# Another order of the same opening steps in a fused windowed-attention and gated-MLP kernel

## The chip, the core and the metric

The kernel runs on one core of a Trainium2 chip. The metric is the device time of one execution in microseconds (us). Three runs of the kernel before gave 309.06, 309.11 and 309.75 us; their median is 309.11 us. One more execution was recorded by the hardware profiler; its span, from the first to the last instruction, is 306.3 us.

The engines go by short names: PE is TensorE, ACT is ScalarE, DVE is VectorE, POOL is GpSimd, SP is SyncE, which here only issues DMA. Each engine works off its own list of instructions in order, and an instruction waits until what it needs is there. PEld stands for the loading of weights into PE.

## The reference, cut to what matters

Batch is 8, with 8 heads, 576 positions and a head dimension of 64. A position attends to itself and the 63 before it. The result, with heads laid side by side, is x: 4608 rows of 512. Then follows a two-layer block with `g = h * cos(h)` between the layers.

```python
scores = scale * np.matmul(q, k.transpose(0, 1, 3, 2))
rel = pos[:, None] - pos[None, :]
mask = (rel >= 0) & (rel < window)           # window = 64
scores = np.where(mask, scores, -1000000000.0)
scores = scores - np.max(scores, axis=-1, keepdims=True)
attn = np.exp(scores)
attn = attn / (np.sum(attn, axis=-1, keepdims=True) + 1e-09)
attn_out = np.matmul(attn, v)
x = attn_out.transpose(0, 2, 1, 3).reshape(B * S, H * D)
h = x @ w_in                                  # 512 x 2048
g = h * np.cos(h)
out = g @ w_out                               # 2048 x 512
```

## The kernel before, in words

**Tiles.** The 4608 rows of x are worked in nine tiles of 512 rows. A tile needs x (attention for its rows), sixteen blocks of h (128 columns of w_in each, from four products over the four quarters of the 512 inputs), the cosine as a sine with a shifted argument on ACT, the gate `h * sin` on DVE, and then four blocks of 128 output rows, each a sum of sixteen products with w_out. While PE works on the products of tile t, a plan with written times puts the attention of a later batch between them. From tile 1 on (lines 579 to 618) nothing is changed.

**Attention.** The eight heads are taken as four pairs. 64 query positions of one pair are a *unit*: two heads of 64 rows make 128 rows, against two blocks of 64 keys. Up to four units form a *group* that shares one PSUM bank. Groups 0 to 7 are batch 0, pair p and half g (n = 2p + g); group 8 is the last block of positions of batch 0; groups 9 to 18 are batch 1. Groups 9 to 16 are needed for tile 1, two for each pair; 17 and 18 for tile 2.

**The opening.** Everything up to the end of tile 0, and the attention of batch 1 beside it, is not planned but written out as a list of steps, `FIRST` (line 50). Its order is the order of instructions on each engine; the list is one sequence for all engines, so a step's place counts only against the other steps of its own engine. The last letter of a step picks the engine: `a` ACT, `d` DVE, `p` POOL, `s` SP (a copy by DMA); a last digit of `s`, `h`, `Gs` and `o.0` picks one of five PSUM banks. The names:

- `Lq0.p`, `Lk0.p`, `Lq1.p`, `Lk1.p`: load q or k of batch 0 or 1 for pair p; issued by POOL and converted to bf16 on the way (line 165), except pair 0 of batch 0, which SP loads unconverted (line 171) and `cq`, `ck` convert. `Lq2.c`, `Lk2.c` load pieces of batch 2 (line 182).
- `Lv0.c`, `Lv1.c`: load 128 positions of v of batch 0 or 1 (line 188); `Lwi.i`, `Lwo.i`: a quarter of w_in or w_out (lines 204, 207). All these are issued by POOL.
- `io`, `mk`, `mc`: build the mask, by two steps on POOL (line 143), five small instructions on DVE (147 to 151) and three casts on ACT (155).
- `tq.p`, `tk.p` (batch 0), `Tq.p`, `Tk.p` (batch 1): transposes on PE (line 216, 18 instructions each); `pq`, `pk`, `Pq`, `Pk`: the copy out of PSUM (lines 234, 236, or the copy helper, line 137).
- `s.p.g` scores, `m.p.g` negated row maximum on DVE (319), `e.p.g` exponentials on ACT (336), `i.p.g` reciprocals on DVE (346), `n.p.g` the product with them (353), `w.p.g` transposed weights on PE (364), `c.p.g` their copy out of PSUM. For groups 8 to 18 the same steps are `Gs`, `Gm` (mask added on DVE, 324), `Ge`, `Gi`, `Gn`, then `Gw` and `Gp` (groups 8, 15, 16) or `Gc` (the others), a transposing DMA issued by SP (367).
- `zA`, `zB`, `zC`, `yA`, `yB`, `y`: v also has to lie shifted by 64 rows; these copy halves of the loaded tiles of batch 0 (`z`) and batch 1 (`y`).
- `v.a.g` (403): products of weights with v for pairs 2a, 2a + 1 and half g; `x.a.g`: the copy to x. `V.p`, `X.p` (384): the same for tile 1, pair p.
- `h.g.f` (417): eight products for half g (256 rows) of tile 0 and two blocks of h; `S.g.f` the sine (423), `g.g.f` the gate (429). `h.0.f` needs `x.0.0` and `x.1.0`, and quarter f // 2 of w_in.
- `o.q.m` (436): quarter q of the sum for output rows m; `oc.m` its copy. `tb`, `tb2` change ACT's function table. `ms.p` clears a tile that later batches use (546).

**Buffers that can hold PE up.** Scores, h and outputs share five PSUM banks, one buffer each, so a product into a bank waits for the last reader of what was there. Transposes and attention outputs rotate through three more banks. In tile 1 five blocks of h fit in the banks before the first gate has to free one. Of POOL's loads the ninth waits, in the trace, until the first has landed (`POOL q L165 <- DMA q<-in_q_dram`), and so on.

Of the kernel before, what the change touches and what calls it, by code (L numbers as in the profile page):

```python
# [648 lines left out]
```

## Time and profile before

| | |
|---|---|
| median of three runs | 309.11 us |
| span of the profiled execution | 306.3 us |
| busy: PE, DVE, ACT, POOL | 296.2, 228.5, 234.3, 192.5 us |
| PE waits for its first input until | 4.19 us |
| first product of tile 0's h (`h.0.0`, line 417) | 21.18 us |
| first product of tile 1's h (line 453) | 57.17 us |
| last instructions of PE (line 465) | from 299.90 us |

The profiler gives no time for the profiled execution other than its span: 306.3 us are 2.8 us less than the median of the runs, and what lies before the first and behind the last instruction is not in the trace. Times in the profile are microseconds from the start of the span unless marked ns. A row of the timeline has the start, the length, the engine, the line of the kernel, the operation, output and input, how many instructions were merged, and in brackets how long the engine sat idle before and for whom it waited. A row of a group has the busy time, the mean length of one instruction in ns, and the idle time before them. Matmuls overlap, so a row's length is longer than the distance to the next.

### The profile page before, as it was taken

The page shows a single profiled execution, that of the slowest core. Times are in us where ns is not written, and L with a number is a line of the kernel's source. Part 1 is how long each engine was busy: PE and PEld are TensorE (multiplying, and loading weights), DVE is VectorE, ACT ScalarE, POOL GpSimd, SP SyncE. Part 2 cuts the span into 40 slices and gives each one's busy share as a digit, 9 for nine tenths or more (in the row PEclk, how much of TensorE's full clock was granted, in tenths as well). Part 3 has the DMA queues.
Part 4 walks back from the last instruction along what each step waited for, and adds up shares of the span by engine and source line. Part 5 has one row for each costly group of instructions (what it writes and reads, how often), then busy time and mean ns, then how long its engine had stood idle before and what let it go on. Part 6 is the DMA issues. An engine that isn't in the chain of part 4 may idle for free.

```text
span 306.3 us, 7904 instructions
## 1 busy us (share of the span) xinstructions
PE 296.2 (97%) x2616; PEld 159.0 (52%) x2616; DVE 228.5 (75%) x908; ACT 234.3 (76%) x785; POOL 192.5 (63%) x228
## 2 busy tenths in 40 slices
...
GB/s 146 179 212 192 200 180 130 121 149 191 226 113 116 175 223 80 121 133 232 125 121 137 231 143 104 157 221 148 86 137 107 169 78 141 2 68 71 1 67 70
DMA packets 159945, 42.14 MB, mean 138 GB/s; under 512 B 148256, under 2 KB 155168, under 8 KB 159904
## 3 DMA queue, kind: packets, MB, share of 16 engines
...
HBM read 36.70 MB, written 9.44 MB: 151 GB/s over the span
## 4 chain that ended last, share of the span: by engine, by line
PE 90%; POOL 4%; DMA 2%; DVE 1%; ACT 1%; issue 1%; POOLq 0%; DVEq 0%; ACTq 0%
PE h_ps L453 35%; PE out_ps L609 35%; PE h_ps L417 5%; PE s_ps L303 4%; PE out_ps L436 4%; PE o_ps L384 3%; DMA k<-in_k_dram 2%; POOL w L353 2%; PE tq_ps L219 1%; POOL v L188 1%; PE out_ps L465 1%; PE s_ps L309 1%; PE tw_ps L364 1%; POOL w_in L204 1%; ACT e L336 1%
## 5 line engine op out<-in xcount | busy, mean ns | idle before, releaser
L609 PE MATMUL out_ps<-w_out,gT 128*128 128x512 bf16 x496 | 117.3, 379 | 0.0
L453 PE MATMUL h_ps<-xT,w_in 128*128 128x512 bf16 x512 | 115.3, 379 | 0.3
L595 ACT ACTIVATE sin<-h_ps 128x512 f32<-128x512 f32 x128 | 73.7, 598 | 32.7 <-PE h_ps L453 31.4
L598 DVE TENSOR_TENSOR gT<-h_ps,sin 128x512 bf16<-128x512 f32 x128 | 82.1, 685 | 21.9 <-ACT sin L595 21.2
L336 ACT ACTIVATE e<-s,negm 128x128 f32<-128x128 f32 (+1 forms) x256 | 97.1, 382 | 0.6 <-DVE negm L324 0.6
L353 POOL TENSOR_TENSOR w<-e,rden 128x512 bf16<-128x512 f32 (+1 forms) x74 | 70.0, 962 | 36.6 <-DVE rden L346 18.8
L453 PEld LDWEIGHTS <-w_in 128*128 128x128 bf16 x512 | 48.8, 98 | 54.7 <-issue 0.4
L609 PEld LDWEIGHTS <-gT 128*128 128x128 bf16 x496 | 45.9, 98 | 44.2
L324 DVE CUSTOM_DVE_ANT_0 s<-s_ps,mask 128x128 f32<-128x128 f32 (+1 forms) x256 | 56.4, 279 | 1.7 <-PE s_ps L309 0.9
L336 ACT ACTIVATION_READ_ACCUMULATOR e<-s,negm 128x1 f32 x256 | 48.3, 189 | 0.0
L182 POOL DMA_DIRECT2D q<-in_q_dram x36 | 28.3, 785 | 10.7 <-DMA q<-in_q_dram 4.0
L188 POOL DMA_DIRECT2D v<-in_v_dram x40 | 34.4, 878 | 0.3 <-issue 0.2
L182 POOL DMA_DIRECT2D k<-in_k_dram x36 | 28.2, 783 | 3.9 <-DMA k<-in_k_dram 1.2
L137 ACT COPY out_sb<-out_ps 128x512 f32<-128x512 f32 (+1 forms) x18 | 10.2, 566 | 24.5 <-PE out_ps L609 18.4
L346 DVE RECIPROCAL rden<-den 128x4 f32<-128x4 f32 (+1 forms) x79 | 13.1, 166 | 19.0 <-ACT e L336 18.6
L303 PEld LDWEIGHTS <-qB 128*128 128x128 bf16 x216 | 16.5, 98 | 14.2
L137 DVE CAST xT<-o_ps 128x512 bf16<-128x512 f32 x24 | 15.5, 677 | 10.1 <-PE o_ps L384 10.1
L137 DVE COPY out_sb<-out_ps 128x512 f32<-128x512 f32 x18 | 12.4, 690 | 13.2 <-PE out_ps L609 12.5
L324 DVE DVE_READ_ACCUMULATOR2_ANT negm<- 128x1 f32 x256 | 21.3, 83 | 0.0
L303 PE MATMUL s_ps<-kT,qB 128*128 128x128 bf16 (+1 forms) x216 | 21.2, 216 | 0.0
L137 POOL COPY v<-v 64x1536 bf16<-64x1536 bf16 (+3 forms) x12 | 18.8, 1570 | 0.3
L137 DVE COPY qB<-tq_ps 64x384 bf16<-64x384 bf16 (+1 forms) x40 | 15.6, 390 | 0.4
...
## 6 DMA issues: line engine op xcount, KB each, us to landing
out_dram<-out_sb SPq DMA_DIRECT2D x16, 512.0 KB, 7.5
v<-in_v_dram POOLq DMA_DIRECT2D x32, 128.0 KB, 5.7
...
w_in<-in_moe_w_in_dram POOLq DMA_DIRECT2D x4, 512.0 KB, 8.7
w_out<-in_moe_w_out_dram POOLq DMA_DIRECT2D x4, 512.0 KB, 10.8
wT<-w SPq DMA_TRANSPOSE x68, 4.4
q<-in_q_dram POOLq DMA_DIRECT2D x7, 144.0 KB, 6.0
```

The lines of the kernel that those rows point to most:

```text
L137: {"a": nc.scalar.copy, "p": nc.gpsimd.tensor_copy}.get(engine, nc.vector.tensor_copy)(out, in_)
L182: nc.gpsimd.dma_start(out=st[name, b][:, c].rearrange("p (h d) -> p h d", h=H), in_=src.rearrange("h p d -> p h d"))
L188: nc.gpsimd.dma_start(out=vt.rearrange("p (h d) -> p h d", h=H), in_=v[b, :, c * 128:c * 128 + n, :].rearrange("h p d -> p h d"))
L303: nc.tensor.matmul(out=s_ps[:, u, 0:64 * chunks].rearrange("p (a t) -> p a t", a=chunks), lhsT=qblocks[(b % 2) * PAIRS + p][:, j].rearrang ...
L324: nc.vector.tensor_tensor_reduce(out=s[:, u, c], in0=s_ps[:, u, c], in1=mask[:, 2 - j % 2 if j else 0, c], scale=-scale if b else -1.0, sc ...
L336: nc.scalar.activation(e[:, u, c], s[:, u, c], AF.Exp, bias=negm[:, u:u + 1], scale=1.0 if n < n_first else -1.0, accum_out=den[:, u:u + 1])
L353: (nc.gpsimd if engine == "p" else nc.vector).tensor_tensor(out=w[:, 0:u], in0=e[:, 0:u], op=ALU.mult, in1=rden[:, 0:u].unsqueeze(2).to_br ...
L417: nc.tensor.matmul(out=h_ps[:, half * e:half * e + half], lhsT=w_in_sb[:, ks, ff * 128:ff * 128 + 128], rhs=st["xT", 0][:, ks, half * g:ha ...
L453: nc.tensor.matmul(out=st["h", ff], lhsT=w_in_sb[:, ks, ff * 128:ff * 128 + 128], rhs=st["xT", mt][:, ks], start=start, stop=stop)
L595: nc.scalar.activation(sin, h_ps, AF.Sin, bias=math.pi / 2.0)
L598: nc.vector.tensor_tensor(out=gt[:, e], in0=h_ps, in1=sin, op=ALU.mult)
L609: nc.tensor.matmul(out=o_ps[e], lhsT=gT[ff // 2][:, ff % 2, ms * 128:ms * 128 + 128], rhs=w_out_sb[:, ff], start=ff == 0, stop=ff == n_ff - 1)
```

## The change

Only the list `FIRST` differs; it takes one line less, so every later line has a number smaller by one in the kernel after. The list holds the same 310 steps; for some the letter or digit at the end differs. In words:

- POOL starts with `Lk0.2 Lk0.1 Lq0.2 Lq0.1`, then `io`, then the other loads of q and k; before, `io` was first and pairs came in order. SP loads k of pair 0 ahead of q, and the q cast follows the mask on DVE.
- Pairs are worked in the order 0, 2, 1, 3.
- Of v only `Lv0.1` and `Lv0.0` come ahead of w_in; the quarters of w_in are loaded in the order 3, 2, 1, 0, and `Lv0.3`, `Lv0.2` follow behind the last. The h steps use the quarters in about that order (h.0.6, 0.5, 0.7, 0.3 and so on), and `v.0.1`, `v.1.1` come behind seven of the eight `h.0` steps instead of behind the third and the fourth.
- The copies `zB`, `zC` of v leave SP's DMA for DVE and POOL; `y.1` goes from DVE to POOL, `yA` from POOL to DVE.
- The clearing of tiles 0, 1, 3, 5, 6, 7 goes from DVE to POOL and to later places. `n.3.0`, `n.2.1`, `n.3.1`, `Gn.8`, `Gn.12`, `Gn.14` go from POOL to DVE, `Gn.17` and `Gn.18` from DVE to POOL. `Pk.3`, `Pq.3`, `Pq.2`, `Gp.8`, `Gp.15`, `oc.0`, among others, go from DVE to ACT, `Pk.0`, `c.1.1` and `x.1.0` from ACT to DVE.
- On PE, scores of groups 11, 13, 14, 8 stand together ahead of the `o` steps; `o.0` for all four row blocks starts early; group 18's scores come before group 16's, and `V.2` is last.

```diff
--- before.py
+++ after.py
@@ -48,27 +48,26 @@
 
 
 FIRST = (
-    "io ms.0.d Lq0.0 Lk0.0 ms.1.d mk cq.d ms.2.d mc ck.a tq.0 Lq0.1 pq.0.d Lk0.1 tk.0 pk.0.a s.0.0.0 "
-    "Lq0.2 tq.1 tk.1 m.0.0 pq.1.a ms.3.d s.0.1.1 Lk0.2 tq.2 pk.1.d s.1.0.2 Lq0.3 Lk0.3 tk.2 s.1.1.3 "
-    "e.0.0 tq.3 m.0.1 Lq1.0 Lk1.0 Lq1.1 pq.2.d pk.2.d Lk1.1 tk.3 m.1.0 s.2.0.4 Lv0.0 Lv0.1 Tq.0 Lv0.2 "
-    "pk.3.d m.2.0 e.0.1 pq.3.a i.0.0 e.1.0 Tk.0 s.3.0.0 Tq.1 e.2.0 Lv0.3 Lwi.0 Pq.0.d i.1.0 Lwi.1 m.3.0 "
-    "m.1.1 i.2.0 Pk.0.a e.3.0 Lwi.2 Tk.1 n.1.0.p s.2.1.1 Pq.1.d Gs.10.2 m.2.1 Gs.9.4 n.0.0.p Pk.1.a "
-    "n.2.0.p i.3.0 e.1.1 w.0.0 zA.0.d w.1.0 c.0.0.d Gs.12.0 w.2.0 n.3.0.p i.0.1 c.1.0.d zA.1.d c.2.0.d "
-    "e.2.1 zB.0.s zB.1.s n.0.1.p i.1.1 w.3.0 v.0.0 c.3.0.d x.0.0.a s.3.1.3 Gm.10 v.1.0 m.3.1 i.2.1 "
-    "Gs.11.2 Gm.9 Gm.12 n.1.1.p x.1.0.a e.3.1 ms.4.d w.0.1 w.1.1 c.1.1.a i.3.1 h.0.0.1 h.0.1.4 tb "
-    "n.2.1.p c.0.1.d Lwi.3 w.2.1 h.0.2.0 n.3.1.p v.0.1 S.0.0 Gm.11 w.3.1 S.0.1 h.0.3.3 Lwo.0 S.0.2 "
-    "c.2.1.d c.3.1.d v.1.1 zC.s g.0.0 S.0.3 h.0.4.2 ms.5.d x.0.1.a x.1.1.d h.0.5.1 g.0.1 h.1.0.4 g.0.2 "
-    "g.0.3 S.0.4 ms.6.d h.0.6.0 h.1.1.3 S.0.5 S.1.0 Lq1.2 S.0.6 g.0.4 S.1.1 g.1.0 h.1.2.2 Lk1.2 ms.7.d "
-    "Lq1.3 h.0.7.4 g.0.5 h.1.3.1 Lv1.0 Lwo.1 g.1.1 S.1.2 h.1.4.3 g.0.6 Lk1.3 S.0.7 h.1.5.0 g.1.2 h.1.6.2 "
-    "Lwo.2 g.0.7 S.1.3 S.1.4 S.1.5 Lwo.3 h.1.7.4 Lv1.1 S.1.6 g.1.3 g.1.4 S.1.7 g.1.5 Lv1.2 g.1.6 tb2 "
-    "Tk.2 Lv1.3 Pk.2.d Ge.10 Tq.2 Pq.2.d Tq.3 Ge.9 Ge.12 o.0.0.1 Pq.3.d Tk.3 o.1.0 Pk.3.d Lv0.4 Lq2.0 "
-    "Ge.11 Gs.14.3 Gi.10 Gm.14 g.1.7 Lq2.1 Gs.13.0 Lq2.2 o.0.1.2 Gi.9 o.2.0 Ge.14 Gn.10.p Gm.13 Gc.10 "
-    "Gi.12 Gs.8.3 o.1.1 Gs.16.4 Gm.8 o.3.0 Ge.13 o.2.1 Gs.15.0 Gi.11 oc.0.d Gn.9.p o.3.1 Gn.12.p o.0.2.3 "
-    "Gi.14 Gm.15 Gs.17.1 oc.1.d Gc.9 Gn.11.p Gi.13 Gm.16 o.1.2 Ge.8 Ge.16 Ge.15 y.1.d Gn.14.p yA.p Gi.8 "
-    "Gc.12 Gm.17 o.0.3.0 Gi.16 Gn.13.p yB.p Gc.11 Gn.8.p Lq2.3 Lq2.4 Lq2.5 o.2.2 Gn.16.d Gw.8 Gc.14 "
-    "Gc.13 Lk2.0 Gp.8.d o.3.2 Gi.15 Gw.16 Lk2.1 Ge.17 Lk2.2 o.1.3 Gn.15.d V.0 Gp.16.d oc.2.a Gw.15 Gi.17 "
-    "Lk2.3 o.2.3 V.1 Gp.15.d X.0.a Gn.17.d X.1.d V.2 V.3 X.2.a X.3.d Gc.17 o.3.3 oc.3.a Gs.18.4 Gm.18 "
-    "Ge.18 Lk2.4 Gi.18 Gn.18.d Gc.18 Lk2.5 Lv1.4 "
+    "Lk0.2 Lk0.1 Lq0.2 Lk0.0 ck.d tk.0 pk.0.a Lq0.1 io Lk0.3 mk mc Lq0.0 cq.d tq.0 pq.0.a Lq0.3 Lq1.1 tk.2 "
+    "pk.2.d tk.1 pk.1.a Lq1.0 s.0.0.0 m.0.0 Lk1.0 Lk1.1 tq.2 pq.2.a tq.1 pq.1.d e.0.0 s.2.0.1 m.2.0 e.2.0 "
+    "tk.3 pk.3.d s.1.1.2 m.1.1 Lv0.1 Lv0.0 Lwi.3 ms.6.p Lq1.2 s.1.0.3 tq.3 pq.3.a m.1.0 e.1.0 Tq.0 s.0.1.4 "
+    "i.2.0 i.0.0 Pq.0.d s.3.0.0 m.3.0 m.0.1 Tk.0 s.2.1.1 m.2.1 i.1.0 Lwi.2 Lwi.1 n.0.0.p n.2.0.p Pk.0.d "
+    "Tk.1 n.1.0.p ms.0.p Lwi.0 e.1.1 i.1.1 zA.1.d Lv0.3 Tq.1 Pq.1.d s.3.1.3 w.0.0 c.0.0.d n.1.1.p Lv0.2 "
+    "e.3.0 i.3.0 zA.0.d n.3.0.d m.3.1 Lv1.4 Lv0.4 Pk.1.a Gs.12.2 w.1.0 c.1.0.d w.2.0 c.2.0.d w.3.0 e.2.1 "
+    "e.0.1 Gs.10.0 Gs.9.1 v.0.0 x.0.0.a c.3.0.d i.2.1 v.1.0 x.1.0.d Gm.12 Gm.10 i.0.1 n.2.1.d Tq.2 e.3.1 "
+    "i.3.1 w.1.1 n.0.1.p c.1.1.d h.0.6.4 n.3.1.d Gm.9 h.0.5.2 tb Pq.2.a S.0.5 g.0.5 Lq2.3 Lq1.3 Lk1.3 "
+    "Lq2.4 Lwo.1 Lk2.1 Lv1.0 Lk1.2 h.0.7.0 h.0.3.3 S.0.3 w.0.1 c.0.1.d g.0.3 S.0.7 g.0.7 ms.1.p Lwo.0 "
+    "h.0.2.1 S.0.2 w.2.1 h.0.1.2 S.0.1 w.3.1 c.3.1.a h.0.0.3 S.0.0 zB.1.d zB.0.d v.0.1 c.2.1.d v.1.1 g.0.2 "
+    "x.1.1.a x.0.1.d ms.7.p g.0.0 Lwo.2 h.0.4.0 S.0.4 ms.3.p h.1.1.1 Lwo.3 ms.2.d h.1.2.3 S.1.1 g.0.1 "
+    "g.1.1 S.0.6 Lv1.2 S.1.2 g.1.2 h.1.3.2 S.1.3 g.0.4 g.1.3 h.1.7.1 h.1.6.3 S.1.6 g.0.6 g.1.6 S.1.7 g.1.7 "
+    "h.1.0.0 S.1.0 h.1.5.2 S.1.5 g.1.0 g.1.5 Lq2.1 h.1.4.4 Lv1.1 Lv1.3 Lq2.2 Lq2.5 S.1.4 tb2 Ge.12 Tk.2 "
+    "Pk.2.d Tq.3 Tk.3 Pk.3.a Ge.10 Gs.8.3 g.1.4 Gm.8 Gs.14.1 Gs.13.0 Gs.11.2 Pq.3.a Gm.13 o.0.0.4 o.0.3.3 "
+    "o.1.0 o.1.3 Gi.12 Gn.12.d o.0.1.0 Gi.10 Gm.11 Gc.12 Gm.14 o.2.0 Lk2.0 Lk2.2 Gn.10.p Gc.10 o.1.1 Ge.9 "
+    "Ge.11 Ge.13 Gi.9 Gn.9.p Gc.9 Gs.18.2 Gm.18 Gs.16.1 Gm.16 o.2.1 Gi.11 Gn.11.p Gc.11 Ge.8 o.0.2.2 Gi.13 "
+    "Gn.13.p Gi.8 Gn.8.d Gs.15.1 o.2.3 Ge.14 Gi.14 Gn.14.d Gc.14 Gc.13 Gm.15 o.1.2 Ge.16 zC.p Gi.16 "
+    "Gn.16.d Ge.15 o.3.1 o.3.3 o.2.2 Gw.16 Gw.8 Ge.18 Gp.8.a Gi.15 Gn.15.d Gw.15 Gp.16.d Gi.18 yA.d "
+    "Gp.15.a o.3.2 oc.2.a Gs.17.1 y.1.p yB.p Lq2.0 Lk2.5 V.0 X.0.a V.1 X.1.a Lk2.4 Lk2.3 V.3 X.3.a Gm.17 "
+    "Ge.17 ms.5.p o.3.0 oc.1.d V.2 X.2.d Gn.18.p Gc.18 Gi.17 Gn.17.p oc.0.a Gc.17 ms.4.d oc.3.a "
 )
 
 
```

## The prediction

> **What bounds the kernel now.** I read the page first (parts 1 and 2), then the timeline of the first 75 us, engine by engine, because the edit reorders nothing else.
>
> ```profile
> span 306.3 us, 7904 instructions
> PE 296.2 (97%) x2616; PEld 159.0 (52%) x2616; DVE 228.5 (75%) x908; ACT 234.3 (76%) x785; POOL 192.5 (63%) x228
> ```
>
> TensorE (PE) is busy for all but 10.1 us, so a reordered opening pays only through PE's idle time, or costs by adding to it. From tile 1's first product to the end the work is untouched: the question is when tile 1 starts, and whether it starts at full rate. Three stretches of the opening, and the joint to tile 1, in the view of windows (columns: stretch, length, then busy time and count of PE, PEld, DVE, ACT, POOL, then clock and DMA):
>
> ```profile
> 7.15:19.72 12.57, 10.55 (x304) 8.31 (x299) 11.91 (x27) 11.70 (x57) 11.57 (x15) 1.00 1.53 186
> 21.18:36.67 15.49, 15.49 (x172) 13.34 (x170) 14.39 (x44) 12.53 (x28) 12.14 (x16) 1.00 1.27 200
> 38.79:52.49 13.70, 13.48 (x118) 6.12 (x113) 11.62 (x66) 13.70 (x73) 11.40 (x13) 1.00 1.64 158
> ```
>
> Up to 19.72 VectorE (DVE) is the full engine and PE idles 2.02 us; in the sixteen `h` steps PE is full; in the exponentials of batch 1 ScalarE (ACT) is full and PE nearly. The marks that I move are in the timeline (start, length, engine, line):
>
> ```profile
> 1.27 0.53 POOL L143 IOTA mask<- 64x128 f32 x2
> 1.75 0.75 POOL L165 DMA_DIRECT2D q<-in_q_dram  x1
> 4.25 0.55 POOL L165 DMA_DIRECT2D q<-in_q_dram  x1
> 3.68 0.46 DVE L137 CAST q<-rows 128x576 bf16<-128x576 f32 x1 [0.60 <-DMA rows<-in_q_dram]
> 4.19 0.69 PE L216 MATMUL tq_ps<-ident,q 64*64 64x64 bf16 x18 [4.19 <-DVE q L137]
> 7.15 0.69 DVE L319 TENSOR_REDUCE negm<-s_ps 128x4 f32<-128x512 f32 x1 [1.47 <-PE s_ps L309]
> 7.72 0.69 PE L216 MATMUL tk_ps<-ident,k 64*64 64x64 bf16 x18
> 9.30 0.69 DVE L319 TENSOR_REDUCE negm<-s_ps 128x4 f32<-128x512 f32 x1
> 8.69 3.52 POOL L188 DMA_DIRECT2D v<-in_v_dram  x4 [0.21 <-issue]
> 12.18 2.27 POOL L204 DMA_DIRECT2D w_in<-in_moe_w_in_dram  x3
> 19.33 0.39 DVE L137 COPY wT<-tw_ps 128x512 bf16<-128x512 bf16 x1
> 21.18 1.93 PE L417 MATMUL h_ps<-xT,w_in 128*128 128x256 bf16 x16
> 22.49 0.76 ACT L137 COPY wT<-tw_ps 128x512 bf16<-128x512 bf16 x1
> 38.79 0.39 ACT L336 ACTIVATE e<-s,negm 128x128 f32<-128x128 f32 x1
> 53.79 0.40 PE L364 MATMUL tw_ps<-ident,w 128*128 128x128 bf16 x4
> 55.72 0.59 ACT L137 CAST xT<-o_ps 128x512 bf16<-128x512 f32 x1 [1.23 <-PE o_ps L384]
> 57.17 2.76 PE L453 MATMUL h_ps<-xT,w_in 128*128 128x512 bf16 x12
> 59.34 1.28 ACT L595 ACT_TABLE_LOAD   x1
> 60.64 3.04 ACT L595 ACTIVATE sin<-h_ps 128x512 f32<-128x512 f32 x6
> ```
>
> So: first scores reduced at 7.15, first `h` product at 21.18, the last of them out by 36.67 (end of the second window), first exponential of batch 1 at 38.79, last transposed weights (`Gw.15`) at 53.79, tile 1 from 57.17, its first sine at 60.64. The chain of waits adds where tile 1 gets into step, the product that needs the sixth bank:
>
> ```profile
> 62.01 1.89 PE h_ps L453 x8
> ```
>
> **The change part by part.** Landings are from the view of DMA issues (last number: us from issue to landing), the first two loads of POOL's queue, issued at 1.75 and 2.48, the second and the fourth v load (four from 8.69 at 0.88: 9.6 and 11.3) and the third quarter of w_in (three from 12.18 at 0.77: 13.7):
>
> ```profile
> q<-in_q_dram POOLq DMA_DIRECT2D x1, 144.0 KB, 4.7
> k<-in_k_dram POOLq DMA_DIRECT2D x1, 144.0 KB, 5.2
> v<-in_v_dram POOLq DMA_DIRECT2D x1, 128.0 KB, 5.7
> v<-in_v_dram POOLq DMA_DIRECT2D x1, 128.0 KB, 5.6
> w_in<-in_moe_w_in_dram POOLq DMA_DIRECT2D x1, 512.0 KB, 12.3
> ```
>
> Prices are means of groups in the first 75 us (busy, mean ns of one):
>
> ```profile
> L319 DVE TENSOR_REDUCE negm<-s_ps 128x4 f32<-128x512 f32 x8 | 5.4, 685 | 1.7 <-PE s_ps L309 1.5
> L137 DVE COPY kT<-tk_ps 128x576 bf16<-128x576 bf16 x5 | 3.8, 754 | 0.2 <-PE tk_ps L216 0.2
> L137 DVE COPY wT<-tw_ps 128x512 bf16<-128x512 bf16 x9 | 3.7, 410 | 1.5 <-PE tw_ps L364 1.4
> L353 DVE TENSOR_TENSOR w<-e,rden 128x512 bf16<-128x512 f32 x3 | 2.1, 690 | 0.1
> L137 DVE COPY v<-v 64x512 bf16<-64x512 bf16 x2 | 0.8, 394 | 0.0
> L137 DVE COPY v<-v 64x2048 bf16<-64x2048 bf16 x1 | 1.1, 1124 | 0.0
> L429 DVE TENSOR_TENSOR gT<-h_ps,sin 128x512 bf16<-128x512 f32 x16 | 10.1, 677 | 0.4 <-ACT sin L423 0.4
> L546 DVE MEMSET qB<- 128x576 uint32 x8 | 4.3, 538 | 0.6
> ```
>
> *1. Loads and mask (+1.7 at the first maximum).* The steps of the mask (`io`) go behind four loads on POOL, so POOL's loads are issued 0.48 earlier (at 1.27, not 1.75): the first lands at 1.75 + 4.7 - 0.48 = 5.97, the second (`Lk0.1`) at 2.48 + 5.2 - 0.48 = 7.20. Four issues take 4.25 - 1.75 = 2.50, so `io` ends near 1.27 + 2.50 + 0.53 = 4.3, the mask on DVE (1.05, five small instructions) near 5.35, and the cast of q, now behind it, at 5.8 instead of 4.14. That wait is hidden: the first scores `s.0.0` stand on PE behind `tk.1`, which needs the second load. Before, transposes of that kind began at 7.72 and the maximum of the scores behind them at 9.30, 1.58 later. Now 7.25 + 1.58 = 8.83 against 7.15. The casts of the mask and `pq.0` on ACT end near 7.3, 0.8 ahead of need; were that cover gone it would cost one for one.
>
> *2. DVE to the first h product (+1.4).* From its first maximum to the last copy for `v.1.0` DVE did, before, 7 maxima 4.80, 6 copies to qT or kT 4.52, a memset 0.54, 2 v copies 0.79, 4 wT copies 1.64 and 6 small reciprocals: 12.3 without these, 12.57 on the clock. Now: 8 maxima 5.48, 5 copies 3.77, 2 v copies 0.79, a norm moved from POOL 0.69, 4 wT copies 1.64 and 5 reciprocals: 12.4, so about 12.5 on the clock. So the last copy ends at 8.83 + 12.5 = 21.3, not 19.72; `v.1.0` and the copy of x (now DVE) take 1.3 (before 1.46): first product at 22.6, against 21.18. The memsets that leave DVE here bought nothing: two lay ahead of the cast of q, in idle time, and the one in this stretch is replaced by a norm. On POOL a memset lies ahead of `Lq1.2`, one ahead of `Lwi.0`, at something between 0.54 each (DVE's row) and twice that; both loads have other loads ahead of them in the DMA queue, so zero.
>
> *3. The sixteen h steps (+2.5 at their end).* Before they filled 15.49 without a gap. Now they hold one more `w` (0.3) and gaps of 0.8: `h.0.2` takes the bank of `Gs.9`, free after DVE has done ten mask-adds at 0.21 (their starts are 19.64, 19.84, 20.05), two norms, a copy and two reciprocals, 4.2 us after x at 22.6, that is 26.8, when PE is there at 22.6 + 4 x 0.88 + 0.3 = 26.4; `v.0.1` needs three gates, a copy and `zB` twice (1024 columns, between the rows of 512 and 2048, 0.62 each), 26.8 + 3.5 = 30.3, where PE is there at 30.0; some 0.2 for smaller ones. End 22.6 + 16.6 = 39.2 against 36.67. *The loads of v behind w_in:* twelve loads land by 14.8 (9.6 + 5.7 - 0.48), then four quarters, a q and two v. Three quarters took from 11.3 + 5.6 = 16.9 to 13.7 + 12.3 = 26.0, 3.0 each, beside three copies of v by DMA that are gone now. At 3.0 the last v is there at 14.8 + 12.0 + 2.3 = 29.1, with DVE at `zB` at 29.0. So 0.1 at most, and I take 0; with a tenth more for each quarter it is 1.3, kept as the upper end, since w_out stands in the same queue behind it.
>
> *4. From the last h to tile 1 (+3.2).* ACT starts its exponentials 38.79 - 36.67 = 2.1 after PE's end: 41.3. Up to group 15 it has 32 at 13.70 / 36 = 0.38, 12.2; two copies `Pk.3`, `Pq.3` that DVE did before, 1.3; and a wait of 0.9, since `Gm.15` stands on DVE behind `Gn.14.d`, which waits for `Ge.14`: 2.0 of work against 1.15 of `Ge.16` for ACT. That is 55.8; reciprocal, norm on DVE and handing over 1.0: `Gw.15` at 56.8 (53.79 before). Behind it on PE wait two parts of `o` (0.93 each), scores and four `V`, 3.6 in all (3.4 before): tile 1 at 60.4. PE without that wait would be there 1.0 earlier.
>
> *5. Joint (+4.4).* ACT goes on from 55.8 with `Ge.18`, two wT copies at 0.76, four copies of 0.59, `Ge.17`, two copies for the outputs and the table load (1.28), 9.2 us: first sine at 65.0 against 60.64. PE has five banks, 20 products, done near 65.0; the sixth waits, as before, for sine and gate, 62.01 - 60.64 = 1.37: 66.4 against 62.01. From there PE sets the pace again, as it did before.
>
> Sum: 306.3 + 4.4 = 310.7 of span. The median of the runs, 309.11, lies 2.8 above the profiled span; I carry this over: **313.5 us**.
>
> **The clock.** Cold and warm differ in the rows while the granted clock reads 1.00 in both:
>
> ```profile
> 9.55 0.62 PE L293 MATMUL s_ps<-mask,ident 64*64 64x512 bf16 x2
> 10.62 0.38 PE L293 MATMUL s_ps<-mask,ident 64*64 64x512 bf16 x2
> ```
>
> The first slow stretch lasts from 4.19 to about 10.3. In the new order PE has, by step 2, nearly nothing between 15.5 (last scores) and 18.3: gaps of 1.6 and 1.0. [...]
>
> **The rivals.**
> - *The clock falls back in that hole.* 6 us at the slow rate, as at the start, lose 6 x (1 - 0.38 / 0.62) = 2.3: 315.8. [...] Chance 0.08.
> - *Only PE's own delay remains.* ACT keeps up, steps 4 and 5 add nothing to 2.5: 311.6. For it: PE is busy 13.48 of 13.70 there, so ACT leads by little. Chance 0.18.
> - *Faster.* PE's 2.02 idle us up to 19.72 are filled and nothing opens in their place: 307.1. It decides whether DVE's last copy ends before 19.7, which with 12.5 of work needs the first maximum by 7.2, and so the second load 1.6 earlier than any row shows. Chance 0.06.
> - *No difference*, within 0.3% (what a measurement can tell here): the front's loss is made good by the memsets off DVE behind 22 us: 309.1. Chance 0.06.
>
> **How the numbers follow.** The forecast has 0.62, its own range 312.5 to 314.8 (1.3 of late weights up, 1.0 for the `Gw.15` wait down). All rivals but two are slower: 0.88 slower, 0.06 same, 0.06 faster. 310.9 to 315.8 takes in the second rival and the clock's, and leaves out what loses under 1.8 us.
>
> **What would show it.** Right: first L319 (L318 after) near 8.8, first product of L417 (L416) near 22.6, no wait of PE for w_in, PE waits for DVE at `v.0.1` and for a norm at `Gw.15`, first sine of tile 1 near 65. Wrong: that product before 21.5, or a first sine of tile 1 before 62.

## The result, and the profile after

Four runs of the kernel after took 314.26 to 315.19 us, median 314.61; four of the kernel before, beside them, 309.06 to 310.05, median 309.43. The ratio is 1.0174, with a 95% interval of 1.0150 to 1.0198: the new order is 1.7% slower. The forecast was 313.5 us, in a range of 310.9 to 315.8. All ratios here leave out runs more than 1.5% above the fastest of their kernel, which are one run of the second experiment (319.26) and two of the twelfth (316.73 and 319.21).

The profiled execution took 314.26 us, 1.8 more than its span. The head of its page, span and busy times and the row of the granted clock:

```profile
span 312.5 us, 7862 instructions
...
PE 295.0 (94%) x2584; PEld 160.4 (51%) x2616; DVE 229.6 (73%) x902; ACT 237.5 (76%) x791; POOL 198.3 (63%) x231
...
PEclk9979999999999999999999999999999999999999
```

By these rows PE's idle time rose from 10.1 to 17.5 us (312.5 less 295.0). Some 1.5 of this is not idle time: 2584 products of PE stand in this trace and 2616 in that of before, and where a record is missing a gap of about 0.05 us is left (between 103.56 and 103.78, in a row of h products, PE is busy for 0.17 of 0.22). The third slice of the clock's row, 15.6 to 23.4 us, stands at 7 tenths; in the kernel before every slice stood at 9. The windows that answer to the first two of before, then the 3.41 us with the hole in PE's work and the 3.42 us that follow (stretch, length, busy time and count of PE, PEld, DVE, ACT, POOL, then clock and DMA):

```profile
8.53:21.90 13.37, 10.61 (x255) 8.36 (x249) 12.86 (x26) 11.71 (x59) 12.95 (x15) 0.88 1.38 198
23.43:40.98 17.55, 15.78 (x177) 13.71 (x174) 17.03 (x47) 12.53 (x27) 15.62 (x20) 1.00 1.46 157
15.34:18.75 3.41, 1.30 (x33) 0.73 (x25) 3.35 (x6) 3.41 (x19) 3.03 (x5) 1.00 1.23 207
18.75:22.17 3.42, 3.22 (x40) 2.68 (x42) 3.21 (x10) 1.99 (x12) 3.42 (x4) 0.50 1.25 206
```

The sixteen h steps took 15.49 us without a gap before; now they take 17.55 with 1.77 of idle time. The timeline names the places (start, length, engine, line, in brackets the idle time before and its releaser):

```profile
8.53 0.69 DVE L318 TENSOR_REDUCE negm<-s_ps 128x4 f32<-128x512 f32 x1 [0.52 <-PE s_ps L308]
15.93 1.04 POOL L352 TENSOR_TENSOR w<-e,rden 128x512 bf16<-128x512 f32 x1 [0.38 <-DVE rden L345]
16.91 1.06 POOL L545 MEMSET qB<- 128x1152 bf16 x1
16.61 1.50 DVE L136 COPY v<-v 64x512 bf16<-64x512 bf16 x1
18.95 0.53 PE L308 MATMUL s_ps<-kT,qT 64*64 64x128 bf16 x6 [1.71 <-DVE qT L136]
23.43 3.66 PE L416 MATMUL h_ps<-xT,w_in 128*128 128x256 bf16 x32
27.73 1.03 PE L416 MATMUL h_ps<-xT,w_in 128*128 128x256 bf16 x8 [0.41 <-DVE negm L323]
29.83 2.42 DVE L136 COPY v<-v 64x1024 bf16<-64x1024 bf16 x2
32.31 0.77 PE L402 MATMUL o_ps<-wT,v 128*64 128x64 bf16 x32 [1.36 <-DVE v L136]
54.60 3.54 POOL L136 COPY v<-v 64x512 bf16<-64x512 bf16 x3
55.85 1.82 DVE L352 TENSOR_TENSOR w<-e,rden 128x384 bf16<-128x384 f32 x1
57.73 0.57 PE L363 MATMUL tw_ps<-ident,w 128*128 128x128 bf16 x7 [1.09 <-DVE w L352]
58.75 0.40 PE L363 MATMUL tw_ps<-ident,w 128*128 128x128 bf16 x4 [0.45 <-DVE w L352]
62.50 2.76 PE L452 MATMUL h_ps<-xT,w_in 128*128 128x512 bf16 x12
66.12 2.07 ACT L594 ACTIVATE sin<-h_ps 128x512 f32<-128x512 f32 x4
67.50 1.89 PE L452 MATMUL h_ps<-xT,w_in 128*128 128x512 bf16 x7 [0.25 <-DVE gT L597]
```

Three operations of DVE are far longer than the same ones elsewhere. The half copy `zA.1` takes 1.50 us (0.49 and 0.29 for the two in the kernel before), the norm of group 16 (the product of its exponentials with the reciprocals) takes 1.82 (0.73 for one of that form before), and the two half copies `zB` take 2.42 (0.62 each by the forecast). Beside each of them POOL is at work. `zA.1` begins while a norm is running on POOL, 0.30 ahead of POOL's memset, and ends at 18.11, 0.14 after that memset. Each of the three is followed by a wait of PE: 1.71 for the scores of group 12, 1.36 at `v.0.1`, 1.09 at `Gw.16`. In the 3.41 us with the first hole PE is busy for 1.30, and right behind them the granted clock is 0.50 for as long again, while PE is nearly full.

### The profile page after: what moved, and what is told of

Read it like the earlier page. It is cut to its first block, busy times and chain, and to the rows that moved or that the text cites. A ratio compares the mean times of both kernels' runs of the same rounds, so it can differ in the third digit from the quotient of the medians.

```text
span 312.5 us, 7862 instructions
## 1 busy us (share of the span) xinstructions
PE 295.0 (94%) x2584; PEld 160.4 (51%) x2616; DVE 229.6 (73%) x902; ACT 237.5 (76%) x791; POOL 198.3 (63%) x231
## 4 chain that ended last, share of the span: by engine, by line
PE 80%; DVE 7%; ACT 5%; DMA 2%; SPq 2%; issue 2%; POOL 1%; POOLq 0%; DVEq 0%; ACTq 0%
PE out_ps L608 34%; PE h_ps L452 30%; PE s_ps L302 4%; ACT e L335 3%; PE o_ps L383 3%; PE h_ps L416 3%; DMA kT<-k 2%; DVE w L352 1%; DVE v L136 1%; SPq L366 1%; PE s_ps L308 1%; DVE s L323 1%; PE out_ps L464 1%; PE tq_ps L218 1%; PE s_ps L292 1%
## 5 line engine op out<-in xcount | busy, mean ns | idle before, releaser
L608 PE MATMUL out_ps<-w_out,gT 128*128 128x512 bf16 x482 | 114.7, 379 | 0.8 <-issue 0.2
L352 POOL TENSOR_TENSOR w<-e,rden 128x512 bf16<-128x512 f32 (+1 forms) x70 | 67.7, 984 | 32.8 <-DVE rden L345 25.8
L136 DVE CAST xT<-o_ps 128x512 bf16<-128x512 f32 x24 | 15.6, 680 | 12.0 <-PE o_ps L383 11.2
L136 DVE COPY out_sb<-out_ps 128x512 f32<-128x512 f32 x17 | 11.7, 690 | 12.5 <-PE out_ps L608 12.5
L136 POOL COPY v<-v 64x2048 bf16<-64x2048 bf16 (+2 forms) x13 | 20.2, 1560 | 0.4
L136 DVE COPY qB<-tq_ps 64x384 bf16<-64x384 bf16 (+1 forms) x40 | 15.6, 389 | 0.4
```

The source lines that it names most:

```text
L136: {"a": nc.scalar.copy, "p": nc.gpsimd.tensor_copy}.get(engine, nc.vector.tensor_copy)(out, in_)
L352: (nc.gpsimd if engine == "p" else nc.vector).tensor_tensor(out=w[:, 0:u], in0=e[:, 0:u], op=ALU.mult, in1=rden[:, 0:u].unsqueeze(2).to_br ...
L608: nc.tensor.matmul(out=o_ps[e], lhsT=gT[ff // 2][:, ff % 2, ms * 128:ms * 128 + 128], rhs=w_out_sb[:, ff], start=ff == 0, stop=ff == n_ff - 1)
```

## The experiments

Theory A, a guess formed on this trace, where `zA.1` took 1.50 us and ended 0.14 behind POOL's memset: DVE's copies within SBUF, and its norms, cannot run beside some work of POOL; one of the two waits until the other's instruction has ended. The change puts memsets, copies and load issues of POOL beside such copies at three places, and the hole made by the first lets the clock fall. The rivals are that the order of the steps, the loads of v, or POOL's longer queue cause the waits. All ratios are to runs of the kernel before on the same chip.

### The memset away from zA

```diff
-    "Tk.1 n.1.0.p ms.0.p Lwi.0 e.1.1 i.1.1 zA.1.d Lv0.3 Tq.1 Pq.1.d s.3.1.3 w.0.0 c.0.0.d n.1.1.p Lv0.2 "
+    "Tk.1 n.1.0.p Lwi.0 e.1.1 i.1.1 zA.1.d Lv0.3 Tq.1 Pq.1.d s.3.1.3 w.0.0 c.0.0.d n.1.1.p Lv0.2 "
...
-    "Ge.17 ms.5.p o.3.0 ..."
+    "Ge.17 ms.0.p ms.5.p o.3.0 ..."
```

> The changed order with one step moved: the clearing ms.0 on GpSimd, which stood beside the first copy of v (zA.1) on VectorE, goes to the end of the list. Theory A (the copy of v on VectorE and the memset and norm on GpSimd exclude each other while they run): zA.1 takes about 0.5 us instead of 1.50, the wait of group 12's scores for Pq.1 shrinks from 1.71 to about 0.7, the first h product comes near 22.4 instead of 23.43, the time falls by 1.0 to 313.6. Theory B (the copy was slow for another reason, such as late v data): zA.1 stays at 1.5 us and the time at 314.6.

Measured: 313.04 us median (312.26 to 313.79), ratio 1.0122 (1.0056 to 1.0189). The window with the hole (why it begins at 16.34 is said with the last experiment):

```profile
16.34:19.75 3.41, 2.40 (x41) 1.75 (x39) 3.35 (x8) 3.41 (x20) 3.41 (x4) 1.00 1.24 207
```

The timeline:

```profile
14.43 2.14 POOL L352 TENSOR_TENSOR w<-e,rden 128x512 bf16<-128x512 f32 x2
16.21 0.51 DVE L136 COPY v<-v 64x512 bf16<-64x512 bf16 x1
17.76 0.35 PE L308 MATMUL s_ps<-kT,qT 64*64 64x128 bf16 x6 [0.92 <-ACT kT L136]
21.44 3.66 PE L416 MATMUL h_ps<-xT,w_in 128*128 128x256 bf16 x32
27.93 0.88 DVE L136 COPY v<-v 64x1024 bf16<-64x1024 bf16 x2
```

The copy is back at 0.51 us and ends 0.15 behind a norm of POOL, for which it still waited. The wait at group 12 falls by 0.8, the mean granted clock is 0.999 to 1.000 in its four runs (0.988 to 0.995 in the four of the kernel after), and the first h product comes 2.0 earlier. Of these 2.0, 0.4 lie ahead of the copy and have nothing to do with it (it begins at 16.21, not 16.61); 1.6 are the copy and the clock. `zB`, at another time against POOL's issues, takes 0.88 for both, and PE does not wait at `v.0.1`. Tile 1 starts 2.9 earlier (59.60 against 62.50); the span, 310.6, is 1.9 shorter, so 1.0 is lost again behind it. The norm of group 16 still takes 1.82. Theory A holds at the first place in the trace; the interval of the whole time still overlaps that of the kernel after.

### PE filled in the hole

```diff
-            nc.tensor.matmul(out=s_ps, lhsT=ident, rhs=mask16[:, 0:4].rearrange("p u c -> p (u c)"), start=True, stop=True,
-                             skip_group_check=True)
+            for _ in range(9):
+                nc.tensor.matmul(out=s_ps, lhsT=ident, rhs=mask16[:, 0:4].rearrange("p u c -> p (u c)"), start=True,
+                                 stop=True, skip_group_check=True)
```

This is the product that puts the mask of a group into its bank; the repetitions only keep PE busy.

> The changed order, but the mask product that opens group 12's bank is issued nine times instead of once (the later eight repeat the same result, nothing else changes), so that TensorE has some 1.9 us of work in its hole between 16.9 and 18.9. Theory A (the granted clock fell to 0.50 because of the hole, and this cost time): the clock stays at 1.00 up to 23 us, scores and transposes of weights behind the hole run at their warm lengths, the first h product comes near 22.9 instead of 23.43, time 314.0. Theory B (the fall cost nothing, because VectorE sets the pace there): the clock stays at 1.00 but the first h product stays within 0.15 of 23.43. Theory C (the fall has nothing to do with the hole): the clock still shows 0.50 near 19 to 22.

Measured: 315.27 us median (313.97 to 319.26), ratio 1.0181 (1.0103 to 1.0259). Timeline (lines here are one higher for PE):

```profile
22.61 3.66 PE L417 MATMUL h_ps<-xT,w_in 128*128 128x256 bf16 x32
29.09 4.21 DVE L136 COPY v<-v 64x1024 bf16<-64x1024 bf16 x2
33.35 0.77 PE L403 MATMUL o_ps<-wT,v 128*64 128x64 bf16 x32 [3.15 <-DVE v L136]
```

The granted clock stays at 1.00 (1.000 as the mean of each run that the ratio uses) and the first h product comes 0.8 earlier, so in these runs the fall goes with the hole. From the copy `zA.1` on, which takes 1.50 here too and began 0.2 earlier (16.38), the gain is 0.6: that is the price of the fall at this mark. The time gains nothing: `zB`, now earlier, meets POOL's row of load issues and memsets for 4.21 us, and PE waits 3.15 at `v.0.1`. What one collision gives back, the next takes.

### v's last loads ahead of w_in again

```diff
-    "... Lv0.1 Lv0.0 Lwi.3 ms.6.p Lq1.2 ..."
+    "... Lv0.1 Lv0.0 Lv0.3 Lv0.2 Lwi.3 ms.6.p Lq1.2 ..."
```

> The changed order, but the last two loads of v that tile 0 needs (Lv0.3, Lv0.2) go ahead of w_in again, as in the kernel before. Theory A (v was there at 28.1, before VectorE came to zB at 29.8; the 1.36 us that TensorE waits at v.0.1 are VectorE's own work and its exclusion by GpSimd): the wait stays above 1.0 us, the time within 0.5 of 314.6. Theory B (moving w_in ahead of v made v late): the wait at v.0.1 falls below 0.4, time 313.3 or less.

Measured: 314.50 us median (313.77 to 317.12), ratio 1.0190 (1.0100 to 1.0280). Timeline:

```profile
31.35 1.47 DVE L136 COPY v<-v 64x1024 bf16<-64x1024 bf16 x2
32.88 0.78 PE L402 MATMUL o_ps<-wT,v 128*64 128x64 bf16 x32 [0.23 <-DVE v L136]
```

The wait fell to 0.23, as theory B had it, but `v.0.1` begins no earlier, and the time is that of the kernel after, as theory A had it. PE came later by itself: in this execution the clock stood at 0.50 for 6.83 us, from 20.48 to 27.31, and the first 32 h products took 5.19 us, not 3.66. So the trace does not decide between the two, and an interval of 0.9% either way leaves room for a small cost of the loads. What speaks against one is the trace of the kernel after, where v's last load had landed by 28.1 and `zB` began at 29.83.

### y.1 and yA exchanged

```diff
-    "... Gi.13 Gn.13.p ..."
+    "... Gi.13 y.1.d Gn.13.p ..."
...
-    "... Gi.18 yA.d Gp.15.a o.3.2 oc.2.a Gs.17.1 y.1.p yB.p ..."
+    "... Gi.18 Gp.15.a o.3.2 oc.2.a Gs.17.1 yA.p yB.p ..."
```

> The changed order with the engines of batch 1's copies of v as before: y.1 on VectorE (behind the reciprocal of group 13), yA on GpSimd (ahead of yB). Theory A (VectorE's norm of group 16 took 1.82 us instead of 0.73 because GpSimd ran the 2048-column copy y.1 at the same time, and this held Gw.16 and Gw.15): the norm takes 0.75, TensorE's wait of 1.09 at Gw.16 goes, tile 1 starts near 61.5 instead of 62.5, time 313.6. Theory B (the norm was long because its own inputs came late, or ScalarE alone sets the pace there): tile 1 stays at 62.5 within 0.3, time 314.6.

Measured: 313.78 us median (313.29 to 317.68), ratio 1.0174 (1.0087 to 1.0261). Timeline:

```profile
55.20 0.35 ACT L335 ACTIVATE e<-s,negm 128x64 f32<-128x64 f32 x1 [0.85 <-DVE negm L323]
55.86 1.08 DVE L352 TENSOR_TENSOR w<-e,rden 128x384 bf16<-128x384 f32 x1
56.99 0.56 PE L363 MATMUL tw_ps<-ident,w 128*128 128x128 bf16 x7 [0.87 <-DVE w L352]
```

The norm of group 16 falls from 1.82 to 1.08, PE's wait only from 1.09 to 0.87, and tile 1 starts at 61.76, not at the 61.5 that was expected. So most of that wait is not the length of this one norm: the forecast's wait of ACT for `Gm.15` shows here at its full size (0.85; it had said 0.9). The two norms ahead of it on DVE took 1.20 each beside norms on POOL, so collisions may have a part in that wait too; this was not tested. The interval of the time overlaps that of the kernel after.

### zB on ScalarE

```diff
-    "h.0.2.1 S.0.2 w.2.1 ... S.0.0 zB.1.d zB.0.d v.0.1 ..."
+    "h.0.2.1 S.0.2 zB.1.a zB.0.a w.2.1 ... S.0.0 v.0.1 ..."
```

> Kernel after, with the two half copies zB of v on ScalarE, behind the sine of h.0.2, not on VectorE ahead of v.0.1. Theory A (a VectorE copy has to wait while GpSimd works on SBUF, so zB takes 2.42 us for some 0.9 of work): ScalarE takes no part in that, v.0.1 begins some 1.1 to 1.3 earlier than 32.3, the wait of 1.36 us is gone, the last h product ends near 39.8 (41.0 after), tile 1 starts near 61.4 (62.5), 313.4 to 313.8 us against 314.6. Theory B (v.0.1 waits for the last load of v behind w_in, landed at 28.1, or for its bank, and zB only shows it): v.0.1 begins after 32.0 as before, 314.4 or more. The wait of 1.71 at group 12 stays in both.

Measured: 314.31 us median (313.09 to 314.97), ratio 1.0108 (1.0061 to 1.0155), on a chip where the kernel before took 310.46. Timeline:

```profile
30.19 2.11 ACT L136 COPY v<-v 64x1024 bf16<-64x1024 bf16 x2
32.35 0.57 PE L402 MATMUL o_ps<-wT,v 128*64 128x64 bf16 x24 [0.63 <-ACT v L136]
33.31 0.32 PE L402 MATMUL o_ps<-wT,v 128*64 128x64 bf16 x8 [0.39 <-ACT wT L136]
```

In this execution a load of k landed late and the first h product came 0.8 later, at 24.20; counted from it, `v.0.1` begins 0.7 earlier than in the kernel after (8.15 behind it, not 8.88). The wait of 1.36 becomes 1.02 in two parts, because the two copies take 2.11 us on ACT. About half of the expected gain is there; the verdict on the whole time is open, since the interval overlaps that of the kernel after.

### The mask first

```diff
-    "Lk0.2 Lk0.1 Lq0.2 Lk0.0 ck.d tk.0 pk.0.a Lq0.1 io Lk0.3 mk mc ..."
+    "io Lk0.2 Lk0.1 Lq0.2 Lk0.0 ck.d tk.0 pk.0.a Lq0.1 Lk0.3 mk mc ..."
```

> Kernel after, with the two mask steps of GpSimd ahead of its four first loads, as in the kernel before. By the forecast's step 1 the wait of 1.21 us for the cast of q is hidden, since the first scores stand behind tk.1, which needs the second load: the wait goes, the first maximum stays within 0.4 of 8.53 or comes 0.5 later with the loads, 314.3 to 315.2 us. Rival: the wait is real; the first maximum comes at about 7.4, first h product 1.1 earlier than 23.4, about 313.4 us.

Measured: 314.33 us median (314.01 to 317.41), ratio 1.0141 (1.0067 to 1.0215). Timeline:

```profile
7.55 0.69 PE L215 MATMUL tk_ps<-ident,k 64*64 64x64 bf16 x18 [0.80 <-DMA k<-in_k_dram]
9.08 0.69 DVE L318 TENSOR_REDUCE negm<-s_ps 128x4 f32<-128x512 f32 x1 [1.53 <-PE s_ps L308]
```

PE starts on q 0.46 earlier (5.58, not 6.04) and then waits 0.80 for the second load of k; the first maximum comes 0.55 later, not earlier. The forecast's step 1 holds: the wait for the cast of q is hidden behind that load.

### Several memsets late, y exchanged, Gm.15 earlier

```diff
-    "... ms.6.p ... ms.0.p ... ms.1.p ... ms.7.p ... ms.3.p ... Ge.17 ms.5.p ..."
+    "... Ge.17 ms.6.p ms.0.p ms.1.p ms.7.p ms.3.p ms.5.p ..."
...
-    "... Ge.14 Gi.14 Gn.14.d Gc.14 Gc.13 Gm.15 ..."
+    "... Ge.14 Gm.15 Gi.14 Gn.14.d Gc.14 Gc.13 ..."
```

`y.1` and `yA` are exchanged as above.

> Kernel after, with five of GpSimd's memsets (0, 1, 3, 6, 7) moved behind tile 1's attention, y.1 on VectorE and yA on GpSimd, and Gm.15 ahead of the norm of group 14. Theory A: what the forecast missed is VectorE and GpSimd holding each other up at three places (zA.1, zB, the norm of group 16). With GpSimd cleared there first h comes at about 21.4 (23.4 after), v.0.1 waits for nothing, the end of h is near 37.5, the waits for groups 16 and 15 fall from 1.5 in all to below 0.8, tile 1 starts at 58.6 to 59.2, 311.5 to 312.6 us: still slower than before by about 1% or less, by what is left of steps 1 to 3. Theory B (the waits come from the order of the steps itself): above 313.0 us.

Measured: 316.38 us median (315.49 to 318.66), ratio 1.0190 (1.0131 to 1.0249). The waits of PE over the whole execution (engine, line, releaser: us in all, times, longest):

```profile
PE o_ps L383 <- DMA wT<-w: 2.8, 4, 1.6
PE s_ps L302 <- DMA kT<-k: 2.0, 2, 1.7
```

The first h product came at 22.47 and the end of h without a wait at `v.0.1`, but with `Gm.15` ahead the norm of group 14 comes no earlier than in the fourth experiment (53.72 against 53.77), although `Gw.16` begins 1.26 earlier. The norm of group 16 takes 0.76 here, and PE still waits 1.03 for it. With the earlier steps comes the transposing DMA that the `V` steps need: a new wait of 1.6 us at one of them, and 2.0 for keys of batch 2 later. The clock fell here twice, at 17.93 and at 62.30, each time for 3.41 us. The time lies where it was expected if the waits came from the order itself (above 313.0). The remedy failed at least in part for a reason of its own, and for theory A only the first place and `zB` (1.02 us for both, no wait) speak here.

### zA.1 behind zA.0

```diff
-    "... zA.1.d Lv0.3 Tq.1 Pq.1.d ... zA.0.d n.3.0.d ..."
+    "... Lv0.3 Tq.1 Pq.1.d ... zA.0.d zA.1.d n.3.0.d ..."
```

> Kernel after, with the half copy zA.1 of v moved behind zA.0 on VectorE; the memset stays where it is on GpSimd. Theory A: without the copy that waited for the memset, the copy to qT behind it runs at 16.7 instead of 18.1, the scores of group 12 begin at 17.4 to 17.9 instead of 18.95, the hole of PE is under 1.2 us and the granted clock stays at 1.00 from 19 to 22, first h near 21.8 (23.4), 312.9 to 313.7 us. Theory B (the memset costs through GpSimd's own queue: the last quarter of w_in, the next norm and the loads come 1.06 later): first h stays at 23.1 to 23.6 and the time at 314.2 to 315.0.

Measured: 315.50 us median (314.83 to 316.60), ratio 1.0154 (1.0106 to 1.0202). Timeline:

```profile
16.84 1.07 POOL L545 MEMSET qB<- 128x1152 bf16 x1
17.65 2.01 DVE L136 COPY v<-v 64x512 bf16<-64x512 bf16 x2
19.69 1.48 DVE L352 TENSOR_TENSOR w<-e,rden 128x512 bf16<-128x512 f32 x1
18.11 0.35 PE L308 MATMUL s_ps<-kT,qT 64*64 64x128 bf16 x6 [0.94 <-DVE v L136]
21.23 0.61 PE L363 MATMUL tw_ps<-ident,w 128*128 128x128 bf16 x4 [1.99 <-DVE w L352]
```

The scores of group 12 come 0.84 earlier, as theory A has it, though nothing changed in POOL's queue. (The wait of 0.94 that is left ends, as the 0.92 of the first experiment, with ACT's copy of kT; the row names a copy of v that is at work then.) But the block only moved: two v copies together take 2.01 beside the memset and the load issues behind it, the norm on DVE 1.48 (0.67 in the kernel after) beside a norm of POOL that began 0.14 ahead of it, and PE now waits 1.99 for it. In that wait the clock falls at 20.52, for 6.83 us. First h comes at 24.61, later than either theory had it, and the time is above both too. What theory A says of the copy stands here, its figures do not.

### The kernel before with zB on VectorE

```diff
-    "e.2.1 zB.0.s zB.1.s n.0.1.p ..."
+    "e.2.1 n.0.1.p ..."
...
-    "n.2.1.p c.0.1.d Lwi.3 w.2.1 h.0.2.0 n.3.1.p v.0.1 ..."
+    "n.2.1.p c.0.1.d Lwi.3 w.2.1 h.0.2.0 n.3.1.p zB.1.d zB.0.d v.0.1 ..."
```

> Kernel before, with one part of the change alone: the two half copies zB of v leave SP's DMA for VectorE, right ahead of v.0.1. Theory A (a VectorE copy waits for GpSimd's work on SBUF): GpSimd issues loads there from 24.1 on, so the two copies take 0.9 to 2.4 us, v.0.1 on PE begins at 25.0 to 26.5 (24.13 before), and the time rises by 0.5 to 2.0 us. Rival (their size alone counts, 0.3 to 0.6 each, beside other work): within 0.3% of before, and PE does not wait.

Measured: 310.74 us median (310.31 to 311.98) against 309.70 for the kernel before, ratio 1.0038 (1.0015 to 1.0061). Timeline:

```profile
24.78 1.77 DVE L136 COPY v<-v 64x1024 bf16<-64x1024 bf16 x2
26.60 0.44 PE L402 MATMUL o_ps<-wT,v 128*64 128x64 bf16 x16 [0.46 <-DVE v L136]
```

This part of the change, alone, costs 0.4% in the other kernel, with PE waiting 0.46 for `zB`: as theory A has it, and no other part of the change is in it. The first of the two copies ends at 25.85, 0.29 behind a norm of POOL. In this execution a load of k was late and the clock fell besides (0.993); the other nine runs, at 0.999 or more, took 310.31 to 311.26.

### The kernel before with one memset on GpSimd

```diff
-    "... n.3.0.p i.0.1 c.1.0.d zA.1.d ..."
+    "... n.3.0.p ms.7.p i.0.1 c.1.0.d zA.1.d ..."
...
-    "... Lk1.2 ms.7.d "
+    "... Lk1.2 "
```

> Kernel before, with one memset (tile 7) moved from VectorE, where it stands beside full PE at 30.7, to GpSimd behind the norm n.3.0, that is to 18.6 to 19.7, where VectorE copies v (zA.1, 18.45, 0.29 us). Theory A: zA.1 waits for the memset, 1.2 to 1.5 us, the last two wT copies behind it come 0.9 to 1.2 later, first h product at 22.0 to 22.4 (21.18 before), time 0.3 to 1.2 us more than before. Rival (the forecast's price of a memset on GpSimd, zero): zA.1 stays below 0.6, first h at 21.2 and the time as before.

Measured: 310.29 us median (308.69 to 313.04), ratio 1.0009 (0.9976 to 1.0041): no difference. Timeline:

```profile
14.79 4.08 POOL L352 TENSOR_TENSOR w<-e,rden 128x512 bf16<-128x512 f32 x4
18.73 0.29 DVE L136 COPY v<-v 64x512 bf16<-64x512 bf16 x1
18.82 1.21 POOL L545 MEMSET qB<- 128x1152 bf16 x1
```

The copy came 0.09 ahead of the memset, took its usual 0.29 us and ended 0.15 behind a norm of POOL; the memset took 1.21 where it takes 1.06 in the kernel after. So DVE does not always lose. Nor does the later one: in the kernel after the copy came 0.30 ahead of the memset, beside such a norm, and went behind it. Which of the two gets in when the norm ends is not shown by these runs, and theory A's expectation fell for that reason. The first h product came at 22.31, 1.1 later than in the trace of before; 0.44 of it is a wait of PE for a norm that stands behind the memset on POOL, a price that is not zero either.

### The kernel before with its early memset late

```diff
-    "Lq0.2 tq.1 tk.1 m.0.0 pq.1.a ms.3.d s.0.1.1 ..."
+    "Lq0.2 tq.1 tk.1 m.0.0 pq.1.a s.0.1.1 ..."
...
-    "... e.3.1 ms.4.d w.0.1 ..."
+    "... e.3.1 ms.4.d ms.3.d w.0.1 ..."
```

> Kernel before, with the one memset that lies in VectorE's full stretch (tile 3, 7.91, 0.54 us) moved behind the next one, to 23.0, beside full PE. By the forecast's step 2 (VectorE is the full engine from its first maximum to its last wT copy) that copy comes up to 0.54 earlier, first h at 20.6 to 20.9 (21.18 before), 308.5 to 308.9 us for 309.1, faster than both kernels. Rival (PE's own transposes and ScalarE's copies set the pace there): first h within 0.15 of 21.18, time as before.

Measured: 309.94 us median (308.48 to 311.03), ratio 0.9998 (0.9974 to 1.0022): no difference. Timeline:

```profile
14.90 1.29 DVE L318 TENSOR_REDUCE negm<-s_ps 128x4 f32<-128x512 f32 x2 [1.06 <-PE s_ps L308]
```

With 0.54 us less to do, DVE waits 1.06 for PE's scores. PE was late here by itself: in the middle of a set of transposes it sat idle for 1.84 us, for nothing that the profile shows, as it did for 0.92 at the same place in the trace of before, and the first h product came at 21.67, later than either expectation. So in this execution DVE does not set the pace at this place, contrary to the forecast's reading of its first window; whether it would without the longer stall is open. The time does not settle it: a gain of 0.5 us is 0.2%, and lies within the interval.

### Memset 0 late and y exchanged

The edits of the first and the fourth experiment together.

> Kernel after, with memset 0 late and y.1 on VectorE, yA on GpSimd, each of which was tried alone. If their gains add (2.9 and 0.5 at tile 1): first h at 21.4, tile 1 at 58.9 to 59.3, 312.0 to 312.9 us, clock 1.00 from 17 to 23. If PE's hole around 17 (0.7 and 0.9 of waiting) sits at the edge of the clock's fall: granted clock 0.50 from about 18.5, first h near 22.4, tile 1 near 60, about 313.5 us.

Measured: 312.60 us median (311.90 to 319.21), ratio 1.0088 (1.0055 to 1.0121). The window with the hole and the one behind it, in the profiled execution:

```profile
15.36:18.77 3.41, 1.77 (x30) 1.28 (x27) 3.32 (x10) 3.41 (x19) 3.17 (x5) 1.00 1.24 208
18.77:22.18 3.41, 3.41 (x75) 2.81 (x72) 2.56 (x7) 2.91 (x16) 3.41 (x4) 0.50 1.24 205
```

The six runs that the ratio uses, with the mean granted clock of each:

```
us      312.44  311.95  312.63  311.90  313.84  312.57
clock   1.000   1.000   1.000   0.999   0.995   0.995
```

Both expectations came true, in different runs of one kernel. Where the clock holds, the mean is 312.2; where it falls for some 3 us (a mean of 0.995 over 312 us is 3.1 us at 0.50), 313.2. That puts the price of a fall at about 1.0 us, from two runs only, one of which is no slower than the others. In the traces it is 0.75 at the first h product: from `zA.1` to there this execution took 5.98 us, that of the first experiment, without a fall, 5.23.

The hole itself is nearly the same as in the first experiment: two gaps, of 0.7 and 0.9 us. What differs is where it lies. Every fall in these traces lasts 3.41 us or twice that, and the records of the clock in a trace (one trace has none) stand on a grid of such steps, at another phase in each execution (in the kernel after at 11.92, 18.75 and 22.17). Here both gaps lie in one step, 15.36 to 18.77, and PE is busy for 1.77 of it. In the first experiment, where the records of the clock begin at 9.51, a step ends at 16.34, between the gaps: PE is busy 2.51 us of the step up to there and 2.40 of the next, and nothing falls.

About half of the change's 1.7% is recovered. What is left was not taken apart further; the first maximum, at 8.53 against 7.15, is one part of it.

## Why the prediction came out as it did

The direction and the range held, and the forecast named the stages that lose time. The sum was 1.8 us of span too low and its carry-over 1.0 too high, and within the sum the errors of steps 2 and 3 and that of step 5 have opposite signs: that the median came out only 1.1 above 313.5 owes something to luck. What the forecast had not seen is that DVE's copies and norms take longer beside instructions of POOL (1.50 us for 0.49, 1.82 for 0.73). Stage by stage the span grew by 1.4 us up to the first maximum, 0.9 to the first h product, 2.1 in the h steps, 1.0 to tile 1 and 0.9 behind its start.

- **The carry-over was wrong.** Each run's time is 1.7 to 1.8 above its own span (314.26 and 312.5 here). The profiled execution of before, at 306.3, was thus one of about 308.1, not of the median's 309.11; 1.0 of the 2.8 that I carried over was the luck of that execution. Against the sum of 4.4 the span rose by 6.2.
- **Step 1 (+1.7) measured +1.4.** The first maximum came at 8.53, not 8.83, and the mask experiment shows that the wait for q's cast is covered as claimed.
- **Step 2 (first h at 22.6) failed:** 23.43. The stretch began 0.3 earlier than forecast, DVE took 0.9 longer in it, and what follows took 1.5, not 1.3. DVE's work was summed at the lengths that it has when POOL hardly stands in its way: "12.5 on the clock" took 13.4 (8.53 to 21.9), the difference being `zA.1`, 1.50 for 0.49. And "zero" for a memset on POOL counted only POOL's queue. The memset ran 16.91 to 17.97, and the copy ended 0.14 later. This is a pattern: of the 28 half copies `zA` in the fourteen traces 27 end 0.11 to 0.15 us behind the end of an instruction of POOL (a norm, a memset or the issue of a load), while their own lengths go from 0.29 to 1.57; the two of before, from which the forecast took its price, are among them. So the traces show one side held up beside the other, in both directions: DVE lost 1.0 here, about the length of the memset (1.06), and POOL's norm at 19.61 took 1.60 us, not the 1.04 of the row above, while DVE copied and normed. They do not show why, nor who comes first when one already waits: the copy began 0.30 ahead of the memset and went behind it. That DVE is "the full engine" fits the kernel after, busy 12.86 of 13.37 us, with the first h product 1.6 earlier, counted from the copy, once the collision and the fall were gone. In the kernel before, 11.91 of 12.57 looked the same, and taking 0.54 from it gained nothing that could be measured; in the one trace DVE then waited for PE, which had stalled for longer.
- **The clock rival, at 0.08, happened,** in all four runs of the kernel after (0.988 to 0.995), but at 0.6 to 1.0 us, not 2.3: in the profiled execution the slow stretch lasted 3.4 us (18.75 to 22.17), not the 6 taken from the start. What it takes for the clock to fall no row of before shows, and the low chance was the author's estimate: here PE was busy for 1.30 of the 3.41 us ahead of the fall, between gaps, and that did not spare it. In the traces PE was busy 0.66 to 1.77 us of the step's 3.41 ahead of each of the ten falls, and of all the other steps behind the slow start only two have less than 1.77 (1.66 in the second experiment, 1.72 in the seventh). So in these traces falls part from no falls at about half a step of work, and whether a hole of this size led to one went with where the steps lay (1.77 us busy in one step in the twelfth experiment, with a fall; 2.51 and 2.40 in two in the first, with none).
- **Step 3 (+1.1 beyond step 2) was too small by 0.95.** The wait of `h.0.2` came as worked out (0.41 for 0.4) and v's last load, landed by 28.1, cost nothing, as taken. The term of `zB` failed: "0.62 each" took 2.42 for both, and `v.0.1` waited 1.36, not 0.3 (the forecast's three gaps, 0.4, 0.3 and 0.2, add up to 0.9, and it took 0.8). The length of that pair on DVE was 0.88 to 4.21 us over the runs of the new order, by what POOL did beside it; in the kernel after each of the two ends 0.25 behind the issue of a load.
- **Step 4 came within 0.2 in size.** From the end of h to `Gw.15`: 17.8 us measured (40.98 to 58.75), 17.6 forecast. But it was built otherwise: ACT waited only 0.33 for `Gm.15`, and the norm of group 16 made up for it with 1.82 beside three copies of v on POOL. In the fourth experiment the two trade places.
- **Step 5 was too large by 1.0.** From tile 1's start to the sixth product the forecast had 6.0 us and the trace 5.0, about what it was before (4.84). ACT's work from group 15 to the first sine came as forecast (9.4 us for 9.2), but PE came to tile 1 2.1 late and ACT to the sine only 1.1, since ACT ran ahead while PE waited at `Gw.16`. So the first sine began 3.6 behind tile 1's start, not 4.6.
- **Behind the sixth product** the forecast had nothing, and another 0.7 us were lost. The trace names a wait of PE of 0.4 for keys of a later batch by DMA and two of 0.2. Such waits come and go: for keys it is 1.2 us in the tenth experiment, on the kernel before, and nothing in the trace of before itself. Whether the change causes them was not tested.
- **The other rivals:** "only PE's own delay" fell, since PE waited 1.54 at `Gw.16` and `Gw.15`; "faster" needed DVE's last copy before 19.7, and it came at 21.9; "no difference" hoped for gains behind 22 us from the memsets, and there were losses.
